# Scaling k one pair later, with three more places for weights, in a fused attention and feed-forward kernel

## The chip, the cores and the metric

The kernel runs on one core of a Trainium2 chip. The metric is the device time of one execution in microseconds (us), as the median of several runs. The engines are TensorE (PE; its weight loads are shown apart as PEld), VectorE (DVE), ScalarE (ACT), GpSimd (POOL) and SyncE (SP), which here only issues DMA transfers.

## The reference

There are 8 sequences (b), 12 heads, 448 positions and 64 dimensions per head. q and k are normalised by their root mean square, attention is computed, and the result, laid out as 3584 tokens of 768 features, goes through a gated feed-forward layer.

```python
q_n, k_n = rmsnorm(q, g_q), rmsnorm(k, g_k)
scores = q_n @ k_n.T / sqrt(64)
attn = softmax(scores)
x = (attn @ v)                      # 8 x 448 tokens, 12 heads x 64 = 768 features
xn = x / sqrt(mean(x * x) + 1e-6) * rms_g
g, val = xn @ w_gate, xn @ w_val    # 768 -> 1536
out = (g * sigmoid(g) * val) @ w_out  # 1536 -> 768
```

The weights arrive as 64-bit floats, and the kernel converts them to 32-bit itself.

## The kernel before, in words

The kernel has a general path and a path for scores that are known to stay small; these inputs take the second, the function safe_scores. It works on **pairs** of heads: pair g is heads 2·hp and 2·hp + 1 of sequence b, with g = 6·b + hp, and there are 48. The loop over g does the attention of pair g and then a share of the feed-forward work of an earlier sequence.

All five engines run a schedule that is written by hand: each engine executes its instructions in the order in which the Python code issues them. The function pe counts steps (`now["t"]`); `after(n, fn)` puts work off until n steps later; fill issues the next feed-forward items from the list todo, and after each item calls convert once. A block of a pair is: seven score steps (the function step: scores, L638, weighted values, L653, and the exponentials, L643), then a first fill, the transposition of q for the next pair, a second fill, the transposition of k for the next pair, and a third fill. At hp = 0 the order is a fill of three items, q's transposition, one item, rms_x, k's transposition, and then the rest.

**Preparing q and k.** squares takes the squares of pair g + 2 on ACT (L493), DVE sums them (L496, one step later), POOL makes the reciprocal roots (rms_qk, L517 and L518, two steps later) and scales q with them (norm_q, L523). norm_k scales k in place on ACT, in two halves of three instructions each (L531), three and four steps after the squares. turn transposes q (part 0) or k (part 1) on PE (L545, L549); ACT moves q's transpose out (qT, L550), DVE moves k's (kT, L551 and L553). Pairs up to g = 6, called direct, don't scale k: their exponentials take the scale (L567).

**Converting weights.** In the first stage, sequence 0, convert handles one piece of 128 x 384 weights per call, in a pipeline over five calls: the load of the raw 64-bit words (L796), the split on ACT (L809, L810), the join on DVE (L815 to L817), the last addition on POOL (L857), and two calls later the store to DRAM as a 32-bit block (kept, L845). A piece in conversion has its place `top` in the pool cv_pool, which has four; some early pieces use places of another pool (`xs`). A piece's place is free again after its L857.

**Weight blocks.** Converted blocks live in a list of free places, free_w. It starts with NW = 23 and gets two more, former `top` places, when conversion is done. From sequence 1 on, ask loads blocks from DRAM in the order of their use (L955) as long as enough places are free, and used gives a place back. The products follow a Strassen scheme: derive makes differences of gate and value blocks on DVE (L970) and stores them, derive_o does it for the output weights (L991), and derive_q makes the sums of output weights for a second, nested level of the scheme (L1018 to L1021, stored by L1025 and L1028). derive_q does a job only when its two loads were asked for at least wait steps ago. The nested level is used by out_quads (L1340, with its ACT copy L1359 and its DVE additions L1360 to L1381) for sequences 2, 5 and 6.

The products with gate and value weights are L1407 in sequence 0 and L1048 afterwards.

Of the kernel before, what the change touches and what calls it, by code (L numbers as in the profile page):

```python
# [335 lines left out]
def safe_scores(  # L336
# [22 lines left out]
    def pool(name, bufs, **kw):  # L359
        return ctx.enter_context(tc.tile_pool(name=name, bufs=bufs, **kw))  # L360

    NW = 23
    const, small = pool("c_const", 1), pool("c_small", 4)
    qk_pool, v_pool, qn_pool, qkT_pool = pool("c_qk", 3), pool("c_v", 3), pool("c_qn", 1), pool("c_qkT", 2)
    e_pool, tmp, y_pool, rest_pool = pool("c_e", 11), pool("c_tmp", 1), pool("c_y", 3), pool("c_rest", 2)
    x_pool, s_pool, slots = pool("c_x", 4), pool("c_xs", 3), pool("c_slots", 1)
    raw_pool, cv_pool, l2_pool = pool("c_raw", 7), pool("c_cv", 4), pool("c_l2", 5)
    scratch = pool("c_dram", 1, space=DRAM)
    ps_s, ps_m, ps_f = pool("c_ps_s", 4, space=PSUM), pool("c_ps_m", 1, space=PSUM), pool("c_ps_f", 3, space=PSUM)

# [113 lines left out]
    def squares(g, i):  # L484

        if g >= NG:
            return
        n = 2 * NK
        if i == 0:
            st["ms", g] = small.tile([128, 2 * n], F32, name="ms")  # L490
        ms = st["ms", g]
        sq = tmp.tile([128, n * D], F32, name="sq", tag="sq", bufs=2)
        nc.scalar.activation(sq, st["qk", g][:, i], ACT.Square)  # L493

        def reduce():
            nc.vector.tensor_reduce(out=ms[:, i * n:(i + 1) * n], in_=sq.rearrange("p (n d) -> p n d", d=D), axis=AX_X, op=ALU.add)  # L496

        if g <= 1:

            return reduce, lambda: rms_qk(g, slice(i * n, (i + 1) * n))  # L500
        after(1, reduce)
        if i == 1:
            if g == 2:

                due[0:0] = [(now["t"] + 2, lambda: rms_qk(g)), (now["t"] + 2, lambda: norm_q(g))]
                return
            after(2, lambda: rms_qk(g))
            after(2, lambda: norm_q(g))
            if not direct(g):
                for half in range(2):  # L510
                    after(3 + half, lambda half=half: norm_k(g, half))

    def rms_qk(g, cols=slice(0, 4 * NK)):
        if ("rs", g) not in st:
# [11 lines left out]

    def norm_k(g, half):

        for n in range(NK * half, NK * (half + 1)):
            block = st["qk", g][:, 1, n * D:(n + 1) * D]  # L530
            nc.scalar.activation(block, block, ACT.Copy, scale=st["rs", g][:, 2 * NK + n:2 * NK + n + 1])  # L531
# [315 lines left out]
    def convert():  # L847

        n = turn_of["n"]
        if n >= TURNS or not room(1):  # L850
            return False
        turn_of["n"] += 1
        if 0 <= n - 5 < len(pieces):
            key = pieces[n - 5][0]
            st[key] = block()
            lo, top = st.pop(("cv", n - 5))
            nc.gpsimd.tensor_tensor(data(key).bitcast(I32), top, lo, ALU.add)  # L857
        if 0 <= n - 4 < len(pieces):
            st["cv", n - 4] = join(*st.pop(("cv", n - 4)))
        if 0 <= n - 3 < len(pieces):  # L860
            st["cv", n - 3] = split(st.pop(("raw", n - 3)), n - 3)
        if n < len(pieces):
            st["raw", n] = load_raw(pieces[n][1])
        if 0 <= n - 7 < len(pieces):
            keep(pieces[n - 7][0])
        if turn_of["n"] == TURNS:

            free_w.extend(cv_pool.tile([128, BW], F32, name="top") for _ in range(2))
            whole = [raw_pool.tile([128, 2 * BW], F32, name="raw") for _ in range(7)]
            room_so.extend(whole[:6])  # L870
            homes = [whole[6][:, 0:BW], whole[6][:, BW:]] + [cv_pool.tile([128, BW], F32, name="top")[:, :] for _ in range(2)]
            carried.extend(t.rearrange("p (c n) -> p c n", c=KG) for t in homes)
        return True
# [127 lines left out]

    todo_q = list(jobs_q)

    def derive_q(wait=3):

        if not todo_q or len(free_w) < 2:
            return False
        i, j = todo_q[0]
        keys = [("wx", 2, ORDER_Q[i], c) for c in (j, j + KG)]
        for key in keys:  # L1010
            if asked.get(key, now["t"]) > now["t"] - wait:
                return False
        todo_q.pop(0)
        own_a, own_b = ("ta", i, j), ("tb", i, j)
        st[own_a], st[own_b] = block(), block()
        x, y, ta, tb = (data(key).rearrange("p (h n) -> p h n", h=2) for key in (*keys, own_a, own_b))

        nc.vector.tensor_tensor(tb[:, 1], x[:, 1], x[:, 0], ALU.subtract)  # L1018
        nc.vector.tensor_tensor(ta[:, 1], y[:, 1], x[:, 1], ALU.subtract)
        nc.vector.tensor_tensor(ta[:, 0], y[:, 1], tb[:, 1], ALU.subtract)  # L1020
        nc.vector.tensor_tensor(tb[:, 0], y[:, 0], ta[:, 0], ALU.subtract)  # L1021

        def store():
            parts = kept_q[i].rearrange("p (n w) -> p n w", w=HW)
            nc.sync.dma_start(out=parts[:, j], in_=x[:, 0])  # L1025
            for src, first, second in ((y, 1, 6), (ta, 2, 3), (tb, 4, 5)):
                gap = (second - first) * KG
                nc.sync.dma_start(out=parts[:, first * KG + j:second * KG + j + 1:gap], in_=src)  # L1028
            asked["sums_q"] = asked.get("sums_q", 0) + 1

        after(1, store)
        for key in (*keys, own_a, own_b):
            after(3, lambda key=key: used(key))
        return True
# [532 lines left out]
    for g in range(NG + 1):  # L1567
        b, hp = divmod(g, NPAIR)
        if g:
            load_pair(g + 3)  # L1570
        if hp == 2:
            for i in range(2):
                load_rests(b + 1, i, nc.sync)
            load_v_rests(b + 1)
        if g == 0:
            pe(lambda: score(0, (0,)))
            pe(lambda: rests(0))
            pe(lambda: score(0, (1,)))
            pe(lambda: turn(1, 0))
            pe(lambda: score(0, (2,)))  # L1580
            norm_rests(0, 2, 4)
            squares(2, 0)
            squares(2, 1)
            pe(lambda: turn(1, 1))
            for _ in range(3):
                convert()
            load_pair(3)
            load_v(2)
            convert()
            load_rows()  # L1590
            continue
        if g <= NPAIR:
            pe(lambda: score(g, (0,)))
            squares(g + 2, 0)
            squares(g + 2, 1)
            if g > 1:
                pe(lambda: turn(g + 1, 0))
                some_rests(g)
                pe(lambda: turn(g + 1, 1))
            pe(lambda: rests(g))  # L1600
            pe(lambda: values(g - 1))
            if g == 1:
                pe(lambda: turn(g + 1, 0))
                some_rests(g)
                pe(lambda: turn(g + 1, 1))
            load_v(g + 2)

            turns(1 if g == 1 else 3 if g < NPAIR else 0)
            pe(lambda: sums(g - 1))
            pe(lambda: score(g, (1, 2)))  # L1610
            turns(2 if g == 1 else 3 if g == NPAIR else 0)
            if g == 2:
                bound()
            continue

        if g == NPAIR + 1:
            some = lambda *parts: [exps(g, i, scores(g, i)) for i in parts]
            pe(lambda: (rests(g), some(0, 1)))
            pe(lambda: rms_x(0))
            pe(lambda: values(g - 1))  # L1620
            load_v(g + 2)
            pe(lambda: some(2, 3))
            pe(lambda: norm_x(0))
            pe(lambda: some(4, 5))
            pe(lambda: sums(g - 1))
            later_sums(g, 2)
            begin(0, 15)
        else:
            pe(lambda: [step(g, i) for i in (0, 1)])
            pe(lambda: (totals(g - 1), step(g, 2)))  # L1630
            load_v(g + 2)
            pe(lambda: [step(g, i) for i in (3, 4)])
            pe(lambda: ([step(g, i) for i in (5, 6)], weigh(g - 1, 2)))
            if g < NG:
                later_sums(g, 2)
        st["block"] = now["t"]
        if hp:
            fill()
            squares(g + 2, 0)
            squares(g + 2, 1)  # L1640
            pe(lambda: turn(g + 1, 0))
            some_rests(g)
            fill()
            pe(lambda: turn(g + 1, 1))
            fill()
            continue
        fill(3)
        pe(lambda: turn(g + 1, 0))
        fill(1)
        pe(lambda: rms_x(b - 1))  # L1650
        squares(g + 2, 0)
        squares(g + 2, 1)
        pe(lambda: turn(g + 1, 1))
        fill(len(todo))
        begin(b - 1, 16)
        pe(lambda: norm_x(b - 1))
        fill()
# [41 lines left out]
```

## Time and profile before

| | |
|---|---|
| median of 3 runs | 1575.67 us (1574.29 to 1576.02) |
| the profiled execution | 1576.01 us |
| its span | 1573.8 us |
| granted TensorE clock, mean | 0.996 |
| PE busy | 97% |
| DVE, POOL, ACT busy | 62%, 46%, 33% |
| DMA traffic | 327.26 MB, 208 GB/s on average |

The span is the time from the first to the last instruction on the core. Busy shares are of the span. In the profile's lists of waits, a line names the waiting instruction and what released it, then the total in us, the number of times and the longest. In the timeline, a row has the start and the duration in us, and in brackets how long the engine was idle before it and what ended that. A row with x3 merges three instructions. A wait for several things is put down to the one that came last.

### The profile page before, as it was taken

How to read it: one execution, taken by the hardware profiler on the slowest of the kernel's cores; microseconds unless marked ns; L12 is line 12 of the kernel's file. 1: busy time of each engine (PE TensorE's matmuls, PEld its weight loads, DVE VectorE, ACT ScalarE, POOL GpSimd, SP SyncE). 2: the span in 40 equal slices, each digit the busy share in tenths (PEclk: the TensorE clock that was granted, in tenths of full speed). 3: DMA queues.
4: the chain of work that ended last, by engine and by line, in shares of the span. 5: the costliest groups of instructions: out<-in, count | busy, mean ns of one | idle time of the engine just before them, and what ended most of it. 6: DMA issues, size and time to landing. Idle time of an engine off the chain costs nothing.

```text
span 1573.8 us, 25892 instructions
## 1 busy us (share of the span) xinstructions
PE 1531.4 (97%) x8900; PEld 1198.3 (76%) x8900; DVE 982.2 (62%) x1697; ACT 518.3 (33%) x1201; POOL 725.6 (46%) x718
## 2 busy tenths in 40 slices
PE   8899999999999999999999999999999999999997
PEld 4344445687865788888887888768888788899997
DVE  5878889678864566854548544534548545573454
ACT  6756556333332332233332333333332332101000
POOL 6857787654433454464534644345544642021003
PEclk9999999999999999999999999999999999999999
DMA  7656656675889987786557755485456754578665
GB/s 191 208 162 206 212 160 212 213 232 191 280 253 284 304 284 250 251 249 185 167 155 228 238 187 160 146 255 162 148 152 217 226 175 144 156 260 256 175 196 186
DMA packets 314081, 327.26 MB, mean 208 GB/s; under 512 B 84308, under 2 KB 310868, under 8 KB 313940
## 3 DMA queue, kind: packets, MB, share of 16 engines
q1 hardware_dynamic: 313012, 325.31, 66.9%
q8 instruction: 73, 1.20, 0.3%
q14 instruction: 68, 0.56, 0.1%
q10 hardware_dynamic: 800, 0.20, 0.1%
q0 software_dynamic: 128, 0.00, 0.0%
HBM read 271.62 MB, written 53.77 MB: 207 GB/s over the span
## 4 chain that ended last, share of the span: by engine, by line
PE 74%; DVE 5%; issue 3%; POOL 2%; DMA 1%; ACT 0%; SPq 0%; POOLq 0%; DVEq 0%; ACTq 0%
PE ff L1048 41%; PE sc L638 11%; PE ff L1340 9%; PE ff L1272 5%; PE av L653 2%; PE ff L1145 2%; PE ff L1407 2%; PE tr L545 1%; POOL es L681 1%; DVE l L1215 1%; POOL rs L518 0%; DVE raw L1189 0%; DVE w L970 0%; DMA kept_o<-w 0%; DVE raw L1215 0%
## 5 line engine op out<-in xcount | busy, mean ns | idle before, releaser
L1048 PE MATMUL ff<-x,w 128*128 128x224 f32 x1866 | 380.5, 354 | 0.0
L1048 PEld LDWEIGHTS ff<-x,w 128*128 128x128 f32 x1866 | 348.5, 190 | 16.8 <-issue 11.3
L1048 PE MATMUL ff<-xs,w 128*128 128x224 f32 x1392 | 284.7, 353 | 4.4 <-DVE w L970 4.1
L1048 PEld LDWEIGHTS ff<-xs,w 128*128 128x128 f32 x1392 | 261.9, 190 | 6.4 <-issue 5.3
L681 POOL TENSOR_TENSOR es<-es,e 128x448 f32<-128x448 f32 x205 | 243.8, 1189 | 18.0 <-ACT e L643 4.9
L638 PE MATMUL sc<-qT,kT 64*64 64x448 f32 x1176 | 236.9, 546 | 7.7 <-ACT e L643 3.6
L653 PE MATMUL av<-e,vt 64*64 64x448 f32 x984 | 203.7, 545 | 0.0
L643 ACT ACTIVATE e<-sc 128x448 f32<-128x448 f32 x294 | 154.8, 545 | 124.9 <-PE sc L638 107.1
L676 POOL TENSOR_TENSOR es<-e 128x448 f32<-128x448 f32 x41 | 47.3, 1155 | 280.2 <-ACT e L643 280.2
L638 PEld LDWEIGHTS sc<-qT,kT 64*64 64x64 f32 x1176 | 76.4, 134 | 126.4 <-issue 94.2
L670 DVE RECIPROCAL rd<-rd 128x448 f32<-128x448 f32 x41 | 121.0, 2950 | 46.5 <-ACT rd L669 43.7
L531 ACT ACTIVATE qk<-qk,rs 128x64 f32<-128x64 f32 x246 | 65.0, 336 | 180.5 <-POOL rs L518 180.5
L621 POOL TENSOR_TENSOR ss<-ss,rd 128x448 f32<-128x448 f32 x40 | 46.4, 1160 | 157.6 <-ACT rd L620 157.6
L518 POOL TENSOR_TENSOR rs<-ms,mhalf 128x12 f32<-128x12 f32 (+1 forms) x50 | 115.5, 2310 | 4.2
L1060 DVE TENSOR_TENSOR cc<-ff,u 128x448 f32<-128x448 f32 x84 | 52.4, 624 | 99.7 <-PE ff L1048 98.0
L1340 PE MATMUL ff<-w,l 128*128 128x192 f32 x578 | 109.9, 329 | 3.4 <-DVE l L1215 2.3
L1407 PE MATMUL ff<-x,w 128*128 128x448 f32 x288 | 111.8, 541 | 0.0
L1340 PEld LDWEIGHTS ff<-w,l 128*128 128x128 f32 x578 | 95.4, 190 | 9.1 <-DVE l L1215 3.8
L1407 PEld LDWEIGHTS ff<-x,w 128*128 128x128 f32 x288 | 53.3, 190 | 51.0 <-issue 49.8
L1312 POOL TENSOR_TENSOR y<-y,c 128x384 f32<-128x384 f32 x10 | 12.2, 1218 | 161.7 <-DVE y L1381 157.7
L1060 DVE TENSOR_TENSOR u<-ff,p 128x448 f32<-128x448 f32 x42 | 26.2, 624 | 87.5 <-PE ff L1048 85.5
L857 POOL TENSOR_TENSOR w<-top,raw 128x384 int32<-128x384 int32 x63 | 65.8, 1055 | 30.9 <-issue 8.3
(204 smaller groups left out, 2396.3 us busy)
## 6 DMA issues: line engine op xcount, KB each, us to landing
w<-kept SPq DMA_DIRECT2D x512, 192.0 KB, 3.4
w<-kept_q SPq DMA_DIRECT2D x323, 192.0 KB, 3.6
w<-kept_o SPq DMA_DIRECT2D x136, 192.0 KB, 3.8
kept<-w SPq DMA_DIRECT2D x91, 192.0 KB, 3.9
kept_q<-w SPq DMA_DIRECT2D x57, 192.0 KB, 3.4
qk<-in_q_dram SPq DMA_DIRECT2D x48, 192.0 KB, 3.6
qk<-in_k_dram SPq DMA_DIRECT2D x96, 96.0 KB, 3.5
raw<-in_moe_w_gate_dram SPq DMA_DIRECT2D x24, 384.0 KB, 4.8
```

Source lines behind the costliest of these rows:

```text
L518: nc.gpsimd.tensor_tensor(st["rs", g][:, cols], ms, mhalf[:, cols], ALU.pow)
L638: nc.tensor.matmul(ps[r, 0:S], lhsT=st["kT", g][r, keys_of(i)], rhs=st["qT", g][r, :], start=True, stop=True)
L643: nc.scalar.activation(e, ps[:, 0:S], ACT.Exp)
L653: nc.tensor.matmul(st["av", g][own(j), 0:S], lhsT=vt, rhs=st["e", g, i][r], start=i == 0, stop=i == PARTS - 1, skip_group_check=True)
L670: nc.vector.reciprocal(rd, rd)
L681: nc.gpsimd.tensor_tensor(st["es", g], st["es", g], st["e", g, i], ALU.add)
L857: nc.gpsimd.tensor_tensor(data(key).bitcast(I32), top, lo, ALU.add)
L1048: nc.tensor.matmul(bank[:, w * HT:(w + 1) * HT], lhsT=wt[:, c * 128:(c + 1) * 128], rhs=x[:, c, :], start=onto is None and w == c == 0, st ...
L1060: nc.vector.tensor_tensor(add[name], ps[:, 0:S], add[other], ALU.add)
L1272: nc.tensor.matmul(ps, lhsT=left_o(b, which, LEFT_O[name], c), rhs=data(("wo", b, name, c)), start=first and c == 0, stop=c == NFP - 1, sk ...
L1340: nc.tensor.matmul(ps, lhsT=a[:, j, :], rhs=data(key)[:, n % 2 * HW:(n % 2 + 1) * HW], start=start and j == 0, stop=j == KG - 1, skip_grou ...
L1407: nc.tensor.matmul(bank[w][:, 0:S], lhsT=data(key)[:, c * 128:(c + 1) * 128], rhs=st["x", 0, half][:, c, :], start=half == c == 0, stop=ha ...
```

## The change

Four edits. First, norm_k is no longer put off from squares for pair g + 2; it is called in the block for pair g + 1, one half ahead of q's transposition and one half right behind it. Pair 7 has its scaling at the end of the turn for pair 5. Second, cv_pool has six places instead of four, and four of them become weight blocks after conversion instead of two. Third, NW is 24 instead of 23. Fourth, derive_q asks for loads that are four steps old instead of three.

```diff
-    NW = 23
+    NW = 24
...
-    raw_pool, cv_pool, l2_pool = pool("c_raw", 7), pool("c_cv", 4), pool("c_l2", 5)
+    raw_pool, cv_pool, l2_pool = pool("c_raw", 7), pool("c_cv", 6), pool("c_l2", 5)
...
             after(2, lambda: rms_qk(g))
             after(2, lambda: norm_q(g))
-            if not direct(g):
-                for half in range(2):
-                    after(3 + half, lambda half=half: norm_k(g, half))
...
     def norm_k(g, half):
 
+        if g >= NG:
+            return
         for n in range(NK * half, NK * (half + 1)):
...
-            free_w.extend(cv_pool.tile([128, BW], F32, name="top") for _ in range(2))
+            free_w.extend(cv_pool.tile([128, BW], F32, name="top") for _ in range(4))
...
-    def derive_q(wait=3):
+    def derive_q(wait=4):
...
             if g == 2:
                 bound()
+            if g == NPAIR - 1:
+                for half in range(2):
+                    norm_k(g + 2, half)
             continue
...
         if hp:
             fill()
+            norm_k(g + 1, 0)
             squares(g + 2, 0)
             squares(g + 2, 1)
             pe(lambda: turn(g + 1, 0))
+            norm_k(g + 1, 1)
             some_rests(g)
             fill()
             pe(lambda: turn(g + 1, 1))
             fill()
             continue
-        fill(3)
+        fill(2)
+        norm_k(g + 1, 0)
+        fill(1)
         pe(lambda: turn(g + 1, 0))
+        norm_k(g + 1, 1)
         fill(1)
         pe(lambda: rms_x(b - 1))
         squares(g + 2, 0)
```

## The prediction

> **What bounds the kernel now.** I read the page's busy line first, then PE's waits, then ACT's, then the timeline at each long PE wait.
>
> ```profile
> PE 1531.4 (97%) x8900; PEld 1198.3 (76%) x8900; DVE 982.2 (62%) x1697; ACT 518.3 (33%) x1201; POOL 725.6 (46%) x718
> ```
>
> TensorE is busy 1531.4 of 1573.8 us, and the change removes no matmul. It can only touch some 42 us of gaps, plus time at a lower clock. Who ends the gaps (total us, times, longest):
>
> ```profile
> PE ff L1048 <- DVE w L970: 4.1, 2, 2.6
> PE sc L638 <- ACT e L643: 3.6, 2, 2.2
> PE ff L1340 <- DVE cc L1360: 3.2, 3, 1.1
> PE sc L563 <- ACT e L567: 3.0, 2, 2.3
> PE sc L638 <- DVE kT L553: 2.8, 1, 2.8
> ...
> PE sc L638 <- ACT rd L669: 1.3, 1, 1.3
> ```
>
> ACT is only 33% busy, yet it is late for PE. Its own waits say why:
>
> ```profile
> ACT qk L531 <- POOL rs L518: 180.5, 40, 8.9
> ...
> ACT top L809 <- POOL w L857: 7.7, 3, 5.3
> ```
>
> L531 is the scaling of k. In 40 of 41 pairs it stands at the head of ACT's queue until POOL has made the roots `rs`, and everything behind it stands too. The timeline at 150, 210 and 664 us (start, duration, in brackets the idle time before):
>
> ```profile
> 147.54 0.82 ACT L531 ACTIVATE qk<-qk,rs 128x64 f32<-128x64 f32 x3 [6.86 <-POOL rs L518]
> 148.27 0.54 ACT L809 ACTIVATE top<-raw 128x384 f32<-128x384 f32 x1
> 148.91 0.84 DVE L815 TENSOR_SCALAR top<-top 128x384 f32<-128x384 f32 x1 [1.72 <-ACT top L809]
> 152.05 0.54 DVE L553 COPY kT<-tr 128x384 f32<-128x384 f32 x1
> 152.65 0.59 PE L638 MATMUL sc<-qT,kT 64*64 64x448 f32 x2 [2.75 <-DVE kT L553]
> 208.91 0.56 ACT L809 ACTIVATE top<-raw 128x384 f32<-128x384 f32 x1 [5.34 <-POOL w L857]
> 211.88 0.95 ACT L643 ACTIVATE e<-sc 128x448 f32<-128x448 f32 x2
> 212.45 1.01 PE L638 MATMUL sc<-qT,kT 64*64 64x448 f32 x2 [2.23 <-ACT e L643]
> 664.06 0.82 ACT L531 ACTIVATE qk<-qk,rs 128x64 f32<-128x64 f32 x3 [8.93 <-POOL rs L518]
> 664.79 0.29 ACT L1359 COPY th<-ff 128x192 f32<-128x192 f32 x1
> 665.12 0.36 DVE L1360 TENSOR_TENSOR cc<-ff,th 128x192 f32<-128x192 f32 x1 [2.00 <-ACT th L1359]
> 665.53 1.24 PE L1340 MATMUL ff<-w,h 128*128 128x192 f32 x6 [1.06 <-DVE cc L1360]
> ```
>
> At 150 the roots hold a conversion's split (L809), that holds DVE's join, and kT is queued behind the join. At 210 a split waits for one of four `top` places that POOL has not freed, and the exponentials are queued behind it. At 664 (again at 854 and 1212) the roots hold a 0.29 us copy in a quarter-block product. One more, for the last edit:
>
> ```profile
> 543.60 0.36 DVE L1018 TENSOR_TENSOR w<-w 128x192 f32<-128x192 f32 x1 [3.65 <-DMA w<-kept_o]
> 547.32 0.59 PE L638 MATMUL sc<-qT,kT 64*64 64x448 f32 x2 [1.30 <-ACT rd L669]
> ```
>
> Here DVE stands on a load that has not landed; a tanh, then `rd`, then PE follow.
>
> [...] the 0.29 us copy comes out only after the 8.93 us wait. [...] the granted clock was 0.53 in 212.40 to 215.90 and 0.71 in 80.50 to 84.00, and score pairs took 0.96 us against 0.54; [...] L970 takes 0.55 us, and up to 1.49 while POOL adds.
>
> **The change, part by part.** From the two built programs: PE and POOL issue the same operations in the same order, apart from the names of weight places. ACT, DVE and SP are reordered; no count changes.
>
> *k scaled later.* The 246 scalings stay (groups of three take 0.83 us). They now come after `rs` is a pair old, so the 180.5 us of ACT waiting go. What each gap on PE gives:
> - 664, 854, 1212: the copy runs when its product ends, about 1 us sooner; 3 × 1.06 = 3.2, I take 3.1.
> - 150: the 1.72 us of DVE idle and 1.25 us of the same kind at 122.96 go; 2.97 against a gap of 2.75. I take 2.4.
> - 75.5 (pair 5): 4.16 us of ACT waiting stand before three splits and the exponentials for which PE waits 2.26. They go; but the six scalings (1.54 us) now follow four exponentials and precede the transposition of pair 7's k. Exponentials from 74.3 (four at 0.55), scalings to 78.0, PE there by 77.1: about 0.95 of new wait. Net 1.3. The half-clock stretch from 79.1 follows this gap; at most 1.7 (half of 3.4), I take 0.9.
>
> The new wait: the transposition of k needs ACT's second group. Queued behind that on PE are the fill items and the next pair's scores. On ACT the group follows qT's eviction (0.63), so it ends 0.63 + 0.83 = 1.46 us after q's transposition. In the trace k's transposition starts 2.8 us after that in five pairs (19, 25, 31, 37, 43), 3.3 at pair 13, 4.3 at 8 and 12, and 5.6 or more (mostly 6.6) in the others: zero, covered by fill items and rms_x. Without the cover it is 0.83 each. qT itself may come 0.83 later where ACT was already 0.7 to 1.3 us late (pairs 18, 23, 29, 35, 39, 42), with DVE's L551 behind it. Bound 0 to 6 × 0.83 = 5.0; pair 42 was 1.33 late with no PE gap, so I take 0.5. Bounds of this part: a gain of 3.2 + 2.75 + 2.26 + 1.7 = 9.9, a loss of 5.0.
>
> *Two more conversion places.* With six, a split waits for an addition (L857) two pieces older. At 208.9 the first two splits run early and the third behind the first of POOL's four additions, not the third (each 1.0 us), so the exponentials gain about 2 us: 2.0 of 2.23 at 210, 1.2 of 1.40 at 183. The half-clock stretch after 210 (1.7) goes with it, I take 1.5. POOL's adds and SP's raw loads keep their order.
>
> What is late next: between 105 and 213 DVE is busy 96.5 of 108 us and waits 7.3 for splits. With PE gaps of 6.4 gone, 101.6 us remain for 96.5 of DVE work. kT was only 1.5 and 1.6 us early at pairs 10 and 11. A gap of some 1 us in two or three of these pairs is likely: I give back 2.5, bounds 0 and 7.1. Stage: 2.4 + 1.2 + 2.0 + 1.5 − 2.5 = 4.6.
>
> *One more weight block.* After conversion 24 + 4 = 28 places instead of 25. In b=1 the differences (L970, with their stores on SP) are made earlier for column blocks 1, 2 and 5, where PE has no gap. For 3 and 4, where the 4.1 us lie (370 and 394.7 us), eight L970 still stand together in DVE's order just ahead of the product, slowed by POOL's adds. So 0. Bounds: −4.1, and +2 if deeper prefetch crowds the queue (DMA share 0.84 to 0.97 in 400 to 560 us). SP waits on PE for a place (228.2 us) get shorter; nothing else changes there.
>
> *Output sums a step later.* Four DVE operations (0.35 us) and four stores on SP move per job. The job at 543.6 now has loads six steps old instead of three and four: the 3.65 us wait goes, and PE's 1.30 with it; I take 1.2. The stores come a step later among the same loads on SP; the last sums are asked for more than 20 steps after they are stored, so no load waits for them. L1018's other waits (6.1 and 5.0 us) cost PE nothing before. Bounds: −1.3 and +1, another wait of this kind.
>
> Sum: 3.1 + 1.3 + 0.9 + 4.6 + 1.2 − 0.5 = **10.6 us**. The profiled execution took 1576.0 us (span 1573.8 and 2.2 around it), which gives 1565.4. It lies 0.3 above the median of 1575.67, so against the runs: **1565.1 us**.
>
> **The rivals.**
> - *DVE takes over in the conversion stage* (0.17): its 4.6 and the early clock's 0.9 don't come, nor is the 0.5 paid; 3.1 + 1.3 + 1.2 = 5.6 remain: 1570. For it: DVE is 89% busy there. Against: 7.3 us of DVE's idle time is the very wait that goes.
> - *The same, and qT late in six pairs* (0.08): 5.6 − 5.0 = 0.6, so 1575, no change. Against: pair 42.
> - *k becomes late for its transposition* (0.06), the slow side: ACT is so far behind that PE waits out a scaling group, 0.83 us, in half of the 40 pairs: +16.6 − 10.6, 1582. It decides from 13 pairs on (13 × 0.83 = 10.8). For it: the transposition had no wait on a recent ACT operation before. Against: qT started within 0.04 us of the transposition's end in most pairs from 12 on, and the cover is 2.8 us at the least.
> - *More than listed* (0.07): nothing is given back, both half-clock stretches go whole, and the differences lose half of their 4.1: 10.6 + 2.5 + 1.0 + 2.0 = 16.1, so 1559.5.
>
> **How the numbers follow.** The likeliest case, 0.62, is 1565.1, of itself 1561.5 to 1568.5 (the stage's 7.1 or 1). From 1559.5, the best case, to 1572.5, just above DVE's, the range leaves out the slow and the unchanged case and a little of each end, some 0.18. A measurement of this kernel can tell about 0.2% (3.2 us) from no change: faster 0.62 + 0.17 + 0.07 = 0.86, same 0.08, slower 0.06.
>
> **What would show it.** Right: ACT waits of L531 on POOL near zero; PE's waits on DVE cc L1360, on `rd` L669 and on e L643 gone; those on L970 unchanged near 4; no half-clock stretch at 212; DVE above 93% busy in 105 to 207. Wrong: PE waiting on ACT qk ahead of the transposition of k, on kT in several pairs, or a new DVE wait for loads in 430 to 630 us.

## The result and the profile after

The changed kernel takes **1558.3 us** (median of 4 runs, 1558.07 to 1559.2) against 1575.85 us of the kernel before beside it: ratio 0.989, 95% interval 0.9873 to 0.9907. The profiled execution took 1558.21 us, its span is 1556.4. The forecast had the direction right, and the stops that it counted on went or became shorter; the 17.5 us gained are 7 more than the sum, and the time is 1.2 us below the low end of the range.

Engines, waits of PE and of ACT in the profile after (us in total, times, longest). Lines of the kernel move up by one or three: L1048 is now L1047, L638 is L637, L643 is L642, L970 is L969, L531 is L530, L518 is L515, L809 is L808, L857 is L856.

```profile
PE 1525.7 (98%) x8900; PEld 1196.4 (77%) x8900; DVE 985.8 (63%) x1697; ACT 516.0 (33%) x1201; POOL 732.1 (47%) x718
```

```profile
PE ff L1047 <- DVE w L969: 4.1, 2, 2.7
PE ff L1339 <- DVE l L1214: 2.3, 5, 1.2
...
PE ff L1047 <- DVE cc L1059: 1.0, 1, 1.0
PE tr L544 <- DVE kT L550: 0.8, 1, 0.8
```

```profile
ACT top L808 <- POOL w L856: 19.4, 6, 5.9
```

The 180.5 us in which ACT stood on `rs` have gone, and with them PE's waits on `cc` L1360, on e L643 (0.4 us is left), on kT L553 and on `rd` L669. The differences' 4.1 us stay, as forecast. Two small waits have grown: on `cc` (L1060, now L1059) from 0.3 to 1.0 us, on kT (L551, now L550) from 0.4 to 0.8. ACT's wait for a place has grown from 7.7 to 19.4 us, though two places were added: ACT now comes to its splits early, and waits there instead of in front of `rs`.

The timeline after, in the two pairs of the conversion stage whose stops were shown at 150 and 210 us (start, duration, idle time before):

```profile
141.20 0.55 DVE L552 COPY kT<-tr 128x384 f32<-128x384 f32 x1
...
143.74 0.59 PE L637 MATMUL sc<-qT,kT 64*64 64x448 f32 x2
...
198.49 0.56 ACT L808 ACTIVATE top<-raw 128x384 f32<-128x384 f32 x1 [5.90 <-POOL w L856]
...
199.41 0.96 ACT L642 ACTIVATE e<-sc 128x448 f32<-128x448 f32 x2
...
199.98 0.59 PE L637 MATMUL sc<-qT,kT 64*64 64x448 f32 x2 [0.39 <-ACT e L642]
```

kT is now 2 us early where it was 2.75 late. At 198.5 a split waits for a place as before (5.90 us), but only one split stands between that wait and the exponentials, so PE loses 0.39 us, not 2.23.

The stretch between these, busy us of each engine, as one window:

```profile
98.90:199.60 100.70, 100.70 (x438) 47.99 (x434) 97.12 (x141) 61.01 (x142) 83.12 (x77) 1.00 0.61 192
```

PE is busy the whole 100.7 us, DVE 97.12 of them (96%). This is where 2.5 us should have been given back.

The quarter-block product of pair 27 after (before: 664.06 to 665.53), and the end of pair 7's q with the transposition of its k:

```profile
647.20 0.32 ACT L1358 COPY th<-ff 128x192 f32<-128x192 f32 x1 [4.17 <-DVE u L1371]
...
649.84 0.34 DVE L1359 TENSOR_TENSOR cc<-ff,th 128x192 f32<-128x192 f32 x1
...
650.77 0.49 PE L544 MATMUL tr<-ident,qk 128*128 128x128 f32 x3
...
651.10 0.82 PE L1339 MATMUL ff<-w,h 128*128 128x192 f32 x4
```

```profile
74.96 1.54 ACT L530 ACTIVATE qk<-qk,rs 128x64 f32<-128x64 f32 x6
...
75.42 0.27 PE L548 MATMUL tr<-ident,rest 128*128 128x128 f32 x1
...
75.62 1.27 PE L544 MATMUL tr<-ident,qk 128*128 128x128 f32 x3
```

The copy is out before PE can want it. In pair 7 the six scalings and k's transposition run at the same time: the transposition is stretched to 1.27 us from 0.49, with 0.28 us of idle time of PE in it. That is the new wait, foreseen as 0.95.

**Where the time went, pair by pair.** The difference of the two traces at the end of each pair's q transposition grows by: 1.93 us at the start, 4.10 in pairs 7 and 8, 2.92, 1.63 and 3.41 in pairs 10, 11 and 12, 1.53 in pair 23, and 1.33 to 1.34 in each of 27, 33 and 45. It shrinks by 0.46 in pair 14, 1.20 in 19 and 0.70 in 24. With 0.2 at the end this makes 17.4, the difference of the spans.

### The profile page after: what moved, and what is told of

It reads as the page before. It is cut to its first block, busy times and chain, and to the rows that moved or that the text cites. A ratio compares the mean times of both kernels' runs of the same rounds, so it can differ in the third digit from the quotient of the medians.

```text
span 1556.4 us, 25844 instructions
## 1 busy us (share of the span) xinstructions
PE 1525.7 (98%) x8900; PEld 1196.4 (77%) x8900; DVE 985.8 (63%) x1697; ACT 516.0 (33%) x1201; POOL 732.1 (47%) x718
## 4 chain that ended last, share of the span: by engine, by line
PE 84%; DVE 11%; issue 1%; ACT 1%; POOL 1%; DMA 1%; SPq 0%; DVEq 0%; POOLq 0%; ACTq 0%
PE ff L1047 42%; PE sc L637 12%; PE ff L1339 11%; PE ff L1271 5%; PE ff L1406 3%; PE av L652 3%; PE ff L1144 2%; PE tr L544 2%; DVE top L816 1%; DVE top L815 1%; DVE l L1214 1%; DVE top L814 1%; DVE xs L727 1%; DVE ms L496 1%; PE av L589 1%
## 5 line engine op out<-in xcount | busy, mean ns | idle before, releaser
L1047 PE MATMUL ff<-x,w 128*128 128x224 f32 x1668 | 341.0, 354 | 0.0
L1047 PEld LDWEIGHTS ff<-x,w 128*128 128x128 f32 x1668 | 312.5, 190 | 12.5 <-issue 6.3
L1047 PE MATMUL ff<-xs,w 128*128 128x224 f32 x1362 | 280.2, 354 | 5.1 <-DVE w L969 4.1
L1047 PEld LDWEIGHTS ff<-xs,w 128*128 128x128 f32 x1362 | 257.5, 191 | 7.6 <-issue 5.3
L637 PE MATMUL sc<-qT,kT 64*64 64x448 f32 x1176 | 234.2, 542 | 0.4 <-ACT e L642 0.4
L642 ACT ACTIVATE e<-sc 128x448 f32<-128x448 f32 x294 | 155.3, 546 | 133.9 <-PE sc L637 116.9
L637 PEld LDWEIGHTS sc<-qT,kT 64*64 64x64 f32 x1176 | 76.1, 132 | 117.0 <-issue 95.4
L669 DVE RECIPROCAL rd<-rd 128x448 f32<-128x448 f32 x41 | 121.0, 2950 | 47.9 <-ACT rd L668 47.9
L515 POOL TENSOR_TENSOR rs<-ms,mhalf 128x12 f32<-128x12 f32 (+1 forms) x50 | 117.0, 2341 | 4.2
L1059 DVE TENSOR_TENSOR cc<-ff,u 128x448 f32<-128x448 f32 x84 | 52.3, 623 | 99.0 <-PE ff L1047 95.7
L1339 PE MATMUL ff<-w,l 128*128 128x192 f32 x526 | 100.9, 329 | 3.7 <-DVE l L1214 2.3
L1066 ACT ACTIVATE th<-c 128x224 f32<-128x224 f32 x42 | 16.3, 389 | 233.4 <-DVE c L1059 233.4
L1339 PEld LDWEIGHTS ff<-w,l 128*128 128x128 f32 x526 | 87.0, 190 | 8.3 <-DVE l L1214 3.8
L1406 PEld LDWEIGHTS ff<-x,w 128*128 128x128 f32 x288 | 53.3, 190 | 51.1 <-issue 49.8
L1059 DVE TENSOR_TENSOR u<-ff,p 128x448 f32<-128x448 f32 x42 | 26.2, 624 | 92.6 <-PE ff L1047 87.8
L856 POOL TENSOR_TENSOR w<-top,raw 128x384 int32<-128x384 int32 x63 | 68.4, 1103 | 19.3 <-DVE top L816 7.2
```

Source lines behind the costliest of these rows:

```text
L515: nc.gpsimd.tensor_tensor(st["rs", g][:, cols], ms, mhalf[:, cols], ALU.pow)
L637: nc.tensor.matmul(ps[r, 0:S], lhsT=st["kT", g][r, keys_of(i)], rhs=st["qT", g][r, :], start=True, stop=True)
L642: nc.scalar.activation(e, ps[:, 0:S], ACT.Exp)
L669: nc.vector.reciprocal(rd, rd)
L1047: nc.tensor.matmul(bank[:, w * HT:(w + 1) * HT], lhsT=wt[:, c * 128:(c + 1) * 128], rhs=x[:, c, :], start=onto is None and w == c == 0, st ...
L1059: nc.vector.tensor_tensor(add[name], ps[:, 0:S], add[other], ALU.add)
```

## The experiments

**One edit at a time, and two.** Diffs of k alone and of k with places are against the changed kernel, the others against the kernel before.

*k alone*: the changed kernel with its other edits undone.

```diff
-    NW = 24
+    NW = 23
...
-    raw_pool, cv_pool, l2_pool = pool("c_raw", 7), pool("c_cv", 6), pool("c_l2", 5)
+    raw_pool, cv_pool, l2_pool = pool("c_raw", 7), pool("c_cv", 4), pool("c_l2", 5)
...
-            free_w.extend(cv_pool.tile([128, BW], F32, name="top") for _ in range(4))
+            free_w.extend(cv_pool.tile([128, BW], F32, name="top") for _ in range(2))
...
-    def derive_q(wait=4):
+    def derive_q(wait=3):
```

> The kernel before with k's scaling moved alone; places, weight blocks and derive_q stay as they were. Theory (each edit removes its own gaps on PE, and the sum of 10.6 us was too small where it gave back 2.5 us to DVE): the gaps at 75, 150, 664, 854 and 1212 us go, with the half-clock stretch at 79; those at 183 and 210 stay, since the splits there wait for POOL. That is 4.1 + 2.9 + 4.0 = about 11 us less. Rival (the conversion places carry the conversion stage): only the three gaps of the quarter-block stage go, 3 to 4 us.

Measured 1562.93 us (1561.63 to 1564.79), ratio to before 0.9915, interval 0.9897 to 0.9934. So 14 us of the change come from k alone, 3 more than the theory's 11. The stops at 75 and 150 and all three quarter-block stops are gone by the same amounts as in the whole change. Those at 183 and 210 did not stay as they were: 1.10 and 1.59 us of them remain, with no clock loss behind them, and pairs 11 and 12 gain 0.30 and 2.21 us:

```profile
200.87 0.56 ACT L808 ACTIVATE top<-raw 128x384 f32<-128x384 f32 x1 [5.38 <-POOL w L856]
...
203.83 0.98 ACT L642 ACTIVATE e<-sc 128x448 f32<-128x448 f32 x2
...
204.43 0.59 PE L637 MATMUL sc<-qT,kT 64*64 64x448 f32 x2 [1.59 <-ACT e L642]
```

Three splits (of which the second and third are left out here) stand between the wait and the exponentials, as in the kernel before; with six places it is one.

*Two more places alone.*

```diff
-    raw_pool, cv_pool, l2_pool = pool("c_raw", 7), pool("c_cv", 4), pool("c_l2", 5)
+    raw_pool, cv_pool, l2_pool = pool("c_raw", 7), pool("c_cv", 6), pool("c_l2", 5)
```

> The kernel before with six conversion places instead of four; two of them stay unused after conversion, so the weight blocks are as before. Theory (own gaps): the gaps at 183 and 210 us and the half-clock stretch after 210 go, about 5 us less; the gaps at 75 and 150 stay, since ACT still waits for the roots there. Rival (the places only help once ACT no longer waits for the roots): less than 2 us.

Measured 1576.68 us, ratio 0.9998 (0.9989 to 1.0006): nothing, as the rival had it. The trace shows a gain and a loss. The start, earlier by chance (see below), gains 2.05 us, pairs 11, 12 and 23 gain 1.63, 1.89 and 1.53; pairs 7, 8 and 10 lose 2.7 together, to half clock behind stops that the kernel before has too, pair 13 loses 1.25, and pair 14 loses 3.20, by a stop of 1.87 us in which the transposition of k waits for DVE's L551 behind the last joins, and a half-clock stretch after it:

```profile
252.81 0.21 DVE L551 COPY kT<-tr 128x64 f32<-128x64 f32 x1
...
253.07 0.55 PE L545 MATMUL tr<-ident,qk 128*128 128x128 f32 x3 [1.87 <-DVE kT L551]
```

This has the form of the prediction's give-back, in a kernel that does only half of the change. How much of it the two places cause is not shown: blocks and sums together, with four places, has the same stop at 1.35 us, where the kernel before has 0.37.

*k and places together*: the diff of k alone without its second pair of lines, so that six conversion places stay, two of which become weight blocks.

```diff
-    NW = 24
+    NW = 23
...
-            free_w.extend(cv_pool.tile([128, BW], F32, name="top") for _ in range(4))
+            free_w.extend(cv_pool.tile([128, BW], F32, name="top") for _ in range(2))
...
-    def derive_q(wait=4):
+    def derive_q(wait=3):
```

> Edits: k scaled later and six conversion places instead of four; 23 weight blocks and the sums' step stay as before. k alone left PE gaps of 1.10 us at 176 and 1.59 us at 203, both behind an exponential that stood behind a split waiting for a place; places alone were worth 0.2 us. Theory (the two edits share one stage: each alone leaves the other's wait, so the places pay only where k has been moved): both gaps go, 2.7 us less than k alone, 1560.2 us, ratio to before 0.990, no half-clock stretch in the conversion stage, PE without a gap there. Rival (places are worth nothing with either order): 1562.9, as k alone, new gaps or half-clock stretches taking the place of the two.

Measured 1561.29 us (1559.98 to 1561.5), ratio 0.9899 (0.988 to 0.9919), 1.6 us under k alone where 2.7 was expected; the intervals overlap, so the times alone do not separate the two theories. The trace does: of the stops at 176 and 203 us the first is gone and 0.37 us of the second is left (1.33 and 1.22 us gained in pairs 11 and 12 against k alone), 2.8 us over the whole conversion stage, as the theory had it. Outside that stage 1.2 us are lost in pair 19, in a half-clock stretch that k alone does not have, and 1.3 in pair 23, at a load (see below). So the places do pay, once k has been moved.

*More weight blocks alone*: four conversion places and 26 blocks, which makes the same 28 places after conversion.

```diff
-    NW = 23
+    NW = 26
```

> The kernel before with 28 places for weight blocks after conversion instead of 25 (NW = 26, the pool of conversion places as before). Theory: no change within 0.1%, since the PE gaps at 370 and 395 us stay: eight differences still stand together in DVE's order ahead of the product. Rival (deeper prefetch carries a part of the 17.5 us): 2 us or more less.

Measured 1580.65 us, ratio 1.0034 (1.0023 to 1.0045): 3.8 us slower by the medians, 5.4 by the ratio. Neither the theory nor the rival had this. The earlier places let derive_q make its sums earlier, and one job lands between the normalisations of x, where POOL adds at the same time (L676 and L681, from 446.69 to 450.50 us). The timeline:

```profile
446.96 1.08 DVE L1018 TENSOR_TENSOR w<-w 128x192 f32<-128x192 f32 x1
447.96 0.34 DVE L1019 TENSOR_TENSOR w<-w,w 128x192 f32<-128x192 f32 x1
448.23 1.28 DVE L1020 TENSOR_TENSOR w<-w,w 128x192 f32<-128x192 f32 x1
449.54 1.17 DVE L1021 TENSOR_TENSOR w<-w,w 128x192 f32<-128x192 f32 x1
450.63 0.67 DVE L711 SCALAR_TENSOR_TENSOR x<-x,rg,rb 128x448 f32<-128x448 f32 x1
...
451.36 1.01 PE L638 MATMUL sc<-qT,kT 64*64 64x448 f32 x2 [3.07 <-DVE x L711]
```

The job of 3.75 us delays the last normalisation; PE waits 3.07 us and then runs a stretch at half clock (0.50 granted from 451.12 to 454.53 us). Together 5.4 us in pairs 19 and 20.

*Sums a step later, alone.*

```diff
-    def derive_q(wait=3):
+    def derive_q(wait=4):
```

> The kernel before with derive_q asking for loads of four steps' age. Theory: the 3.65 us DVE wait for a load at 543 us goes and PE's gap of 1.30 at 546 with it: 1 to 1.5 us less. Rival (the wait goes by the deeper prefetch, not by this edit): no change, the gap at 546 still there.

Measured 1574.62 us, ratio 0.9987 (0.9979 to 0.9995), 2.3 us less. Its trace has no stop at 546 us; but k alone, places alone and blocks alone have none either, without this edit (see below).

*Blocks and sums together*, k and conversion places as before. The blocks are again 26, three more at first and the changed kernel's 28 after conversion.

```diff
-    NW = 23
+    NW = 26
...
-    def derive_q(wait=3):
+    def derive_q(wait=4):
```

> Edits: one more weight block and output weights' sums a step later, k and conversion places as before. Alone they gave +3.8 and -2.3 us. With blocks alone a sums job got between the normalisations of x (L711) at 447 us, 3.9 us long under POOL's adds, and PE waited 3.07 us and then ran 3.4 us at half clock. With the sums a step later that job stands behind them again in DVE's order. Theory (the fourth edit guards the third): the 448 gap and its half-clock stretch go, so 5 us less than blocks alone and the same as sums alone, 1574.6 us within 1.5. Rival (the two add): 1575.85 + 3.8 - 2.3 = 1577.4, with another PE gap behind a sums job.

Measured 1576.48 us, ratio 0.9997 (0.9987 to 1.0006): 4.2 us under blocks alone. The 448 us stop is gone; in DVE's order the job no longer stands between the normalisations. So the fourth edit guards the third, at least in k's old order. It is 1.9 us above sums alone, however, between the two theories' numbers. The trace has half clock behind the stop at 149 us too, where the kernel before has none, and two windows of it behind that at 75; what the traces show of such stretches is in the last section. How much of the 1.9 us that explains is left open, since the times are those of other executions.

**The same kernels again.**

> The kernel before, unchanged, profiled a second time. Theory (some of what differs between two traces is the execution's own and no edit's): the PE gap of 1.30 us at 546 us, which five traces with other edits lack, is absent here too, so that the prediction's 1.2 us for the sums' step were a chance of the one trace; the gaps at 75, 150, 183, 210, 664, 854, 1212 and those of 370 and 394 stay within 0.1 us. [...] the stretches behind 75 and 210 may go or others (behind 150 or 394) come[...]. Rival (the trace of before is repeatable): gap at 546 and stretches at 79 and 212 as before.

One execution, 1575.4 us. The stop at 546 us is there, but smaller:

```profile
542.16 0.36 DVE L1018 TENSOR_TENSOR w<-w 128x192 f32<-128x192 f32 x1 [2.45 <-DMA w<-kept_o]
...
546.19 0.59 PE L638 MATMUL sc<-qT,kT 64*64 64x448 f32 x2 [0.49 <-ACT rd L669]
```

It depends on when the load lands: 1.30 us in the first profile, 0.49 in this one, none in k alone, places alone and blocks alone, 1.04 in k and places together. Neither theory had it so; the prediction's 1.2 us were one draw from this. Of the six traces with loads three steps old three have the stop, of the eight with loads four steps old none: the fourth edit most likely removes it, at a gain that differs from execution to execution. The other stops agree to 0.04 us, and so do both half-clock stretches.

> The changed kernel, unchanged, profiled and timed again. In its first profile TensorE reached full clock at 5.04 us, in the two profiles of before at 10.87 and 10.58 us, which makes 1.9 us of the difference at the first pair; among ten traces of other edits both starts occur without an order. Theory (the start is the execution's own and no edit's): the median stays within 1556.5 to 1560.5 us, and the trace shows full clock from about 5 or about 11 us, with all pairs from 7 to 12, 27, 33 and 45 as in the first profile to 0.1 us, while the half-clock stretch behind 381 us may be there or not. Rival (the changed kernel starts early in itself): full clock at 5 us again, and a median within 0.5 us of 1558.3.

Median 1558.54 us against 1577.51, ratio 0.988 (0.9863 to 0.9896). Its profiled execution took 1561.24 us, and reached full clock at 10.45 us instead of 5.04; three others took 1558.39 to 1558.56. All pairs from 7 to 45 repeat to 0.1 us. So an early or late start is the execution's own: of the 3.0 us between the two profiles of the changed kernel 1.6 lie at the start and 1.3 behind pair 45. Against the first profile of before, which started as late, the second is 14.4 us shorter in span, not 17.4.

**Is DVE the next bound?**

```diff
         nc.vector.scalar_tensor_tensor(top, hi, -(2**30), top, ALU.bitwise_and, ALU.bitwise_or)
+        if 20 <= turn_of["n"] < 60:
+            spare = tmp.tile([128, 64], F32, name="spare", tag="spare", bufs=1)
+            nc.vector.tensor_copy(spare, ones)
```

> The changed kernel with a spare 128x64 copy on DVE behind the join of 40 of the conversion's pieces; the output is untouched. A 128x64 copy (L550) takes 0.21 us in the trace, so 8.4 us of extra DVE work over some 50 us of the stage. In 98.9 to 199.6 us the changed kernel has DVE busy 97.1 of 100.7 us with no PE gap, so about 1.8 us are free in those 50. Theory (DVE is the next bound of the stage, the term given back in the prediction lies just ahead): 8.4 less 1.8 to 3.6 come out as PE gaps, 5 to 6.5 us slower than the changed kernel, 1563 to 1565. Rival (DVE is ahead of PE by buffered pieces and its busy share is stretched by POOL's adds, so that the extra work fits): under 1.5 us slower, 1558.3 to 1559.8.

Measured 1566.7 us, 8.4 above the changed kernel, more than the theory's 5 to 6.5. The 40 copies took 18.5 us, not 8.4, and were spread over 136 us, not 50: 15 of them took over 0.4 us, the longest 1.14. DVE's busy time, counted from 88 us to the end of the same stage, rose by 7.5 us (131.07 in 136.5 us against 123.61 in 129.6; other DVE work shrank), and pairs 8 to 14 are 6.9 us longer. PE's waits on both kT copies and on the exponentials are back:

```profile
PE tr L544 <- DVE kT L550: 3.0, 3, 2.2
PE sc L637 <- DVE kT L552: 2.3, 2, 1.8
...
PE sc L637 <- ACT e L642: 1.5, 1, 1.5
```

Nearly all of what DVE has to do more comes out as longer time. So the changed kernel has little room left before DVE takes over in this stage. The copies also stand ahead of kT's copies in DVE's order; whether it is their length or their place that costs PE is not separated.

**The price of the slow rival.** Both groups of scalings stand right ahead of k's transposition, behind the fill item:

```diff
         if hp:
             fill()
-            norm_k(g + 1, 0)
             squares(g + 2, 0)
             squares(g + 2, 1)
             pe(lambda: turn(g + 1, 0))
-            norm_k(g + 1, 1)
             some_rests(g)
             fill()
+            norm_k(g + 1, 0)
+            norm_k(g + 1, 1)
             pe(lambda: turn(g + 1, 1))
```

In the full blocks likewise, behind `rms_x`.

> The changed kernel with both scaling groups of k behind the fill item and right ahead of k's transposition, so that the cover which the prediction named is gone; nothing else changes. Theory (the price of the slow rival is real, and only the cover keeps it away): in some 40 pairs PE waits at the transposition for ACT to finish the fill item's own operation and six scalings (1.54 us), 1.5 to 2.5 us each, some followed by 3.4 us at half clock: 60 us slower than the changed kernel at least, 1620 to 1680. Rival (ACT runs far enough ahead, or another engine's work fills the wait): under 0.8 us a pair, at most 1590.

Measured 1588.9 us (1585.81 to 1590.4), ratio to before 1.0076 (1.0059 to 1.0093): 30.6 us slower than the changed kernel. PE's waits, and one of them in the timeline:

```profile
PE tr L544 <- ACT qk L530: 14.0, 12, 2.0
```

```profile
139.13 0.54 ACT L1414 ACTIVATE th<-ff 128x448 f32<-128x448 f32 x1 [2.64 <-PE ff L1406]
139.57 0.54 ACT L808 ACTIVATE top<-raw 128x384 f32<-128x384 f32 x1
140.02 0.53 ACT L809 ACTIVATE raw<-raw 128x384 int32<-128x384 uint32 x1
140.46 1.52 ACT L530 ACTIVATE qk<-qk,rs 128x64 f32<-128x64 f32 x6
...
141.08 0.80 PE L544 MATMUL tr<-ident,qk 128*128 128x128 f32 x2 [1.99 <-ACT qk L530]
```

The fill item's own tanh and a split stand ahead of the scalings. Against the changed kernel that costs 2.3 us in each of pairs 10 to 13, and as much again, with a half-clock stretch, in three of them (0.50 granted from 142.17 to 145.59 us in one); 1.1 us in pair 17 and 1.9 in each of six later pairs. The other 29 pairs pay 0.3 us or nothing. So the price of a pair is the theory's and the total the rival's. The sign holds: without the cover the change would have lost to the kernel before.

**Two attempts at a better version.** First, both scaling groups ahead of the step's first fill item:

```diff
         if hp:
+            norm_k(g + 1, 0)
+            norm_k(g + 1, 1)
             fill()
-            norm_k(g + 1, 0)
             squares(g + 2, 0)
             squares(g + 2, 1)
             pe(lambda: turn(g + 1, 0))
-            norm_k(g + 1, 1)
             some_rests(g)
```

In the full blocks likewise, ahead of `fill(3)`.

> The changed kernel with both scaling groups of k ahead of the step's first fill item, instead of one ahead of and one behind q's transposition. Theory (after the change qT comes late in a pair or two because a scaling group of 0.83 us stands ahead of qT's eviction on ACT, as before the PE gap of 0.98 at 552 us; scaled earlier, it stands in time in which ACT waits for PE): the gap at 552 and the 0.7 us of pair 24 go, k's transposition at pair 7 is not later than in the changed kernel, 1557.3 us. Rival (the groups now stand ahead of the exponentials and copies of the fill item, on which PE waits sooner): new PE gaps behind ACT in 5 or more of 40 pairs, 0.8 us each, 1562 us or more.

Measured 1559.06 us (1557.25 to 1560.37), ratio 0.9884. The stop at 552 us is back to the 0.28 us of before and pair 24 is 0.70 us shorter, as expected; no new stop behind ACT comes. The profiled execution fell back to half clock from 8.2 to 11.6 us, which adds 1.8 us. The times show no difference from the changed kernel.

Second, the same, with weight differences spread over the step:

```diff
+            if 1 < now["t"] - st["block"] <= 4:
+                derive()
             if now["t"] - st["block"] > 4 and now["t"] != st.get("left_sums"):
```

> The changed kernel, k's scaling ahead of the first fill item (as in the run of k scaled early), and one group of weight differences (L969) allowed per fill item in the middle of a step (second to fourth unit after its block began), so that they don't stand together ahead of the product that needs them. Theory (the 1.44 and 2.67 us at 356 and 381, with the half-clock stretch behind the second, come from eight differences that stand together in DVE's order, slowed by POOL's adds; spread out they end in time): 4.1 us of gaps and up to 1.7 us of clock go, 0.7 at pair 24 too: 1552 to 1554, no PE wait on L969. Rival (DVE has no room there either, or the blocks' loads come later than the differences are asked for): the wait moves to a neighbouring product or to kT, 1557 to 1559.

Measured 1556.78 us (1555.82 to 1557.69), ratio 0.9875 (0.9858 to 0.9891): 1.5 us under the changed kernel's 1558.3, with intervals that overlap. Of the two waits on L969 the first, 1.44 us, is gone; the second is 2.8 us against 2.67, with its half-clock stretch:

```profile
PE ff L1047 <- DVE top L969: 2.8, 1, 2.8
```

So the theory holds for one of the two column blocks. Ahead of the second, DVE still has its differences in a row from 378.5 us, at up to 1.48 us each.

## Why the prediction was wrong in size

Step by step, against the second profile of the changed kernel, which started as late as that of before (the terms from pair 7 to 45 are the same in the first):

- **Three quarter-block stops: 3.1 forecast, 3.95 found.** All three went. Each cost 1.32 us and not its listed 1.06. The other 0.26 stand around the gap: without the stop the next product starts 0.16 us before the transposition's end in the trace (651.10 against 650.77 + 0.49), and right behind the stop six products take 1.24 us (at 665.53 us), the next six 1.14.
- **Pairs 7 and 8: 1.3 + 0.9 = 2.2 forecast, 4.1 found.** The gap of 2.26 went. The half-clock stretch went whole (1.7, of which I took 0.9). The new wait is 0.78 at the most (1.27 less 0.49), of which 0.28 is idle time of PE, and not 0.95, because PE could transpose the first blocks while ACT still scaled the later ones. This makes 3.2 to 3.7; the rest may be loss around the gap, as above, but that is not shown here.
- **Conversion stage: 4.6 forecast, 7.5 found.** The sizes of its positive parts were good: 2.4 forecast for pair 10 against 2.9, 1.2 for 11 against 1.6, 2.0 + 1.5 for 12 against 3.4. Their cause was not: I booked pairs 11 and 12 to the conversion places, but k alone already gives 0.3 and 2.2 of them, with the half-clock stretch, and the places add only 1.3 and 1.2. **The step that failed is the 2.5 given back to DVE**: 0.5 came, at pair 14. I took 101.6 us of PE work for 96.5 of DVE work and put a gap in two or three pairs for the tightness. In fact 97.1 in 100.7 fit with no gap at all. The spare copies support that the limit lies close, and it was not crossed. From "close to the bound" I made a loss. With 0.5 in place of 2.5 the sum is 12.6 us; the stage's positive parts, the quarter-block stops and pairs 7 and 8 were taken some 3.6 us too small on top of that.
- **Sums a step later: 1.2 forecast, 1.5 found** in the two traces, but that stop varies with a load's landing. As an effect on the median the edit has 2.3 us when alone, of which the interval leaves 0.8 to 3.3 (0.0005 to 0.0021 of 1576 us).
- **qT late: 0.5 forecast, 0.7 found**, in one pair, at 552 us: qT came late at 23, L550 after it, two jobs of sums after that, and then `cc`.
- **Weight blocks: 0 forecast.** The 4.1 us stayed. Alone the edit loses 3.8 us, more than the +2 of my bound, and by DVE's order, not by a crowded queue; that the fourth edit stands guard over it I did not see. In the changed kernel its effect on the trace is none that I can find. The 1.2 us lost in pair 19 are not its own: the stop at 381 us, as long as the old one at 394, now has a half-clock stretch behind it, and k and places together has the same with the old number of blocks.
- **Outside every step:** the start, up to 1.9 us either way, by luck. The median of 1558.3 is that of early starts (1558.07 to 1559.2 us in seven of the eight runs; the one known to have started late took 1561.24). At the other end, behind pair 45, 1.0 us went against the change in the second profile. Only profiled executions show their start, so that the other six started early is argued from their times, not shown. Nor is the start quite apart from the change: the two traces that start early with k's old order (places alone, blocks and sums) gain 2.05 and 2.09 us there and lose 2.7 and 2.8 again in pairs 7, 8 and 10, at half clock behind the stops at 75 and 149, which the changed kernel no longer has.

The rival "DVE takes over" fell; "more than listed" (1559.5) was nearest, for two of its three reasons: nothing much was given back, and the half-clock stretches went whole. The differences' 4.1 us did not move. Effects of the edits do not add: −14.0, −0.2, +3.8 and −2.3 make −12.7 for single edits, against −17.5. The traces say why: places need the moved k, and blocks need the later sums. By the times alone the 4.8 us between the two sums are not much more than their uncertainty.

## What to carry to other kernels

Before you charge a loss for an engine that comes close to its bound, find the instruction that would be late and by how much; close is not crossed, and a spare instruction put on that engine helps to show how far it is. An edit that is worth nothing alone (more buffers) can remove most of a stop once the order in front of it is mended, so cost edits in the state that the others leave. Ask of a moved operation what stands ahead of it in its new place: the same scalings a little later, behind the fill item, would have turned 17 us of gain into 12 of loss.

## What the hardware showed beyond what was expected

**Half clock came behind some stops and not behind others.** Windows of the kernel before, then of the changed one (start and end; us; busy PE, PEld, DVE, ACT, POOL; granted clock; DMA share; GB/s):

```profile
75.72:79.13 3.41, 1.36 (x4) 0.59 (x4) 3.27 (x7) 3.41 (x8) 1.27 (x2) 1.00 0.98 341
79.13:82.55 3.42, 3.42 (x12) 1.65 (x11) 3.39 (x3) 2.53 (x6) 0.00 (x0) 0.50 0.73 223
208.84:212.25 3.41, 1.39 (x12) 0.28 (x4) 2.68 (x3) 3.25 (x7) 3.20 (x4) 1.00 0.69 163
212.25:215.67 3.42, 3.22 (x20) 1.22 (x24) 3.35 (x5) 1.99 (x5) 2.04 (x3) 0.50 1.02 368
...
393.16:396.58 3.42, 1.55 (x10) 1.26 (x9) 3.42 (x4) 2.47 (x5) 3.34 (x3) 1.00 0.81 236
396.58:399.99 3.41, 2.65 (x13) 2.40 (x14) 3.41 (x4) 0.00 (x0) 2.85 (x3) 1.00 1.00 337
```

```profile
380.51:383.93 3.42, 0.75 (x6) 0.52 (x5) 3.42 (x4) 3.19 (x9) 3.26 (x3) 1.00 0.46 167
383.93:387.34 3.41, 3.41 (x10) 3.05 (x11) 3.41 (x5) 0.58 (x3) 2.05 (x2) 0.50 0.32 118
```

The windows are laid out from the clock steps. The end of the kernel from 1540 us on left out, these stand at 10.87, 79.13, 82.55, 212.25 and 215.67 us in the trace of before, and at 5.04, 383.92 and 387.34 us in that of the changed kernel. Each half-clock stretch took 3.41 us, and the later steps lie 20, 21, 59 and 60 times 3.413 us behind the first of their trace, and 111 and 112 times. In the window ahead of the three stretches PE was idle for 2.05, 2.02 and 2.67 us; no other window laid out in this way had more than 1.87 us in these two traces, and none of the others was followed by half clock. In blocks alone the window ahead of the stretch at 451.12 us had 2.83 us of idle time, in the run with both groups behind the fill item that ahead of 142.17 us had 2.29. In places alone, half clock came behind a stop of 1.87 us (at 253.07 us). What makes the clock fall is not shown beyond these cases.

The stop before the second block's product is 2.63 us before and 2.67 after. In the profile of before 1.87 us of it lie in the window from 393.16 us and 0.76 in the next, and the clock stayed at 1.00; in the changed kernel all of it lies in the window from 380.51 us, the clock was 0.50 in the next, and pair 19 lost 1.2 us. That the place of a stop among such windows set its price is my inference from these two. So is that it may cost something else in another execution: the first step came at different times, but the pairs from 7 to 45 of the changed kernel took the same in both profiles to 0.1 us. The quarter-block stops of 1.06 us had no half clock behind them, and each cost 1.32.

The start differs in the same kernel: full clock came at 10.87 and 10.58 us in the two profiles of before, and at 5.04 and 10.45 us in those of the changed kernel. The matmuls show it: at 7.96 us in the first profile of before ten `warm` products took 2.34 us, at 7.42 in that of the changed kernel 1.28. What decides between an early and a late start is not shown.
